# One SBUF side per MLP block, spread table loads and stage-wise schedule offsets in a fused attention, Fourier and MLP kernel

## The chip, the cores and the metric

The kernel runs on one core of one Trainium2 chip. The metric is the device time in microseconds (us), the median of three runs. A profile is one execution recorded by the hardware profiler; its engines are TensorE (PE; PEld is its weight load), VectorE (DVE), ScalarE (ACT), GpSimd (POOL) and SyncE (SP), which only issues DMAs here.

## The reference

Attention with a causal mask and a decay bias, then a block that mixes tokens with a two-dimensional Fourier transform and runs an MLP. All in float32, 8 batches, 8 heads, 576 tokens, 64 columns a head (512 in all), hidden width 2048:

```
scores = scale * q @ k.T                       # per batch and head, 576 x 576
cum = cumsum(max(s, 0));  bias = -(cum[q] - cum[k])
scores = where(causal, -1e9, scores + min(bias, 0))
attn = exp(scores - max); attn = attn / (sum(attn) + 1e-9)
x = attn @ v                                   # (8, 576, 512)
u = x + real(fft(fft(x, axis=1), axis=2))
un = (u - mean(u)) / sqrt(var(u) + 1e-6)       # over the 512 columns
out = u + max(un @ w_ch1, 0) @ w_ch2
```

## The kernel before

**Number format.** Matmuls run on float32 data in a reduced form (F32R). To keep precision a value is held as a high part and a low remainder, and a product takes three matmuls (high by high, high by low, low by high). The function split makes the pair; names ending in h and l, or indices 0 and 1, are its parts.

**Attention.** The 64 heads are worked as 32 pairs; pair i is batch i // 4, heads j = i % 4. For each pair there are steps: load fetches q and k (tile qk); high (L747 to L764) makes the high parts in the tile KQ; low (L776 to L787) makes the remainders q1 and k1 (written as q and k in the profile) and loads the values va; maxes (L802 to L832) computes scores once into pm, takes the row maxima (Mx) on VectorE, transposes them (pmt) and writes them as the row mt back into KQ; scores (L850 to L865) computes the scores ps with maxima and bias inside the product and takes the exponential into P; av (L886 to L898) multiplies by the values (pavA, pavB); recip and finish (L905 to L929) divide by the sums and write x as xa and xs. The loop over pairs interleaves the steps of neighbouring pairs with a function weave, which gives each stream a share.

**Fourier.** After every fourth pair a batch is complete. folds makes even and odd parts (De, Do); fourier multiplies them with cosine and sine tables (pzs, pzc, then pyc, pys) and writes u to DRAM (uD). Its tables are dcos, dsin, scos, ssin, each a high and a low tile, and a correction cor; load_tables (L556 to L562) issues nine transfers from Pool's queue ahead of pair i = 2. After four batches p256 (L660) adds the column 256 by nine matmuls of 290 moving columns.

**Weights.** The weights come as 64-bit numbers; rounded (L389 to L400) turns a piece of them into float32 by a chain over VectorE, ScalarE and Pool, with tiles wm, raw and we. For the first NC = 6 of the 16 blocks convert_w does this during attention and stores the result in DRAM (wD); load_w makes the pair wh, wl of block f, 128 x 1024 each, of which the first 512 columns belong to the first layer and the rest to the second.

**MLP.** The 4608 tokens are nine tiles x = 0 to 8 of 512. ln_tile loads u, gets mean and variance by matmuls with a constant (mu, var), and leaves the centred rows as uch and ucl (L459, L460). mlp_tile runs over the hidden blocks f: twelve matmuls (L497) into h with moving rows uch and ucl, then zh (ScalarE, L501) and zl (VectorE, L502), and for the block before twelve matmuls (L509 to L511) with moving rows zh and zl into four accumulators acc. At a tile's end L528 scales by r = 1 / sqrt(var), L534 to L536 add u back on Pool, and L537 stores. Tiles 0 and 1 are done in halves of eight blocks (parts k = 0 to 3) while later weights are still being made; tiles 2 to 8 are parts k = 4 to 10, each over all 16 blocks.

**Where things lie.** SBUF is given out from two ends; a pool opened with side="right" comes from the far end. Left lie lnp (u, t, th, tl), mlp0 (mu, uch, ucl, r of even tiles), zp (zh, zl), w0 and w1 (weights f < N1 = 8). Right lie, once attention and Fourier are done, wB (weights f >= 8), mlp1 (mu, uch, ucl, r of odd tiles), the stage for the conversion and op (the outputs).

**What sets the order.** The function order rebuilds the order of instructions of the program up to the end of part k = 4. It has a cost for each instruction (function cost), a model of TensorE's clock (class Clock), and times from which first inputs are held to be there (HOLD). It walks in simulated time: at each step an engine may take, of the instructions that could start within SLACK nanoseconds of the soonest, the one of least rank. The rank is the place in the program plus an offset from SHIFT, one number for each engine and name of the tile written. DMAs are held to move one after the other on a line of their issuing queue. The result is fixed as an order on every engine. Parts k > 4 are not reordered by it.

Of the kernel before, what the change touches and what calls it, by code (L numbers as in the profile page):

```python
# [55 lines left out]
SHIFT = {
    (PE, "acc"): 3291, (PE, "h"): 354, (PE, "mu"): -6, (PE, "p"): 8, (PE, "pavB"): 43, (PE, "pyc"): 54, (PE, "pys"): -23, (PE, "pzs"): -13,
    (PE, "var"): 566,
    (DVE, "Aw"): -434, (DVE, "De"): -679, (DVE, "Do"): -601, (DVE, "KQ"): 3, (DVE, "M"): -141, (DVE, "Px"): -20, (DVE, "cumhl"): -44,
    (DVE, "cw"): -401, (DVE, "e"): 160, (DVE, "eh"): 238, (DVE, "eps"): 451, (DVE, "k"): 62, (DVE, "o"): 52, (DVE, "ones"): -453, (DVE, "part"): -15,  # L60
    (DVE, "r"): 323, (DVE, "rows"): -41, (DVE, "sums"): -81, (DVE, "t"): -459, (DVE, "tl"): -439, (DVE, "trash"): -1341, (DVE, "u"): -4312,
    (DVE, "ucl"): -30, (DVE, "wbias"): -672, (DVE, "wl"): -162, (DVE, "wm"): 25, (DVE, "xr"): -154, (DVE, "ym"): -86, (DVE, "yp"): -1168,
    (DVE, "zc"): -17, (DVE, "zs"): -37,
    (ACT, "Do"): 6, (ACT, "KQ"): 2402, (ACT, "P"): 2, (ACT, "Px"): -365, (ACT, "cumhl"): -652, (ACT, "cw"): 15, (ACT, "eh"): 1013, (ACT, "mt"): 6,
    (ACT, "mu"): 59, (ACT, "part"): -533, (ACT, "r"): -28, (ACT, "rows"): -20, (ACT, "stage"): 18, (ACT, "th"): -150, (ACT, "u"): 278,
    (ACT, "we"): -154, (ACT, "yc"): 373, (ACT, "zc"): 4150, (ACT, "zh"): 739, (ACT, "zs"): 66,
    (POOL, "Bw"): -174, (POOL, "KQ"): -43, (POOL, "P"): -36, (POOL, "Px"): -10, (POOL, "dcos"): -18, (POOL, "dsin"): -24, (POOL, "ident"): 1630,
    (POOL, "o"): -72, (POOL, "q"): -5, (POOL, "scos"): -715, (POOL, "ssin"): 102, (POOL, "t"): -374, (POOL, "tri"): -12, (POOL, "trih"): 105,
    (POOL, "w"): -98, (POOL, "we"): 11, (POOL, "wl"): -321, (POOL, "xa"): -123, (POOL, "xr"): -22, (POOL, "xs"): -667,
    (SP, "KQ"): 22, (SP, "aD"): -5, (SP, "cumD"): 48, (SP, "cw"): 558, (SP, "k"): -85, (SP, "out_0_dram"): -113, (SP, "part"): -146, (SP, "qk"): 832,  # L70
    (SP, "raw"): 2317, (SP, "rb"): -1213, (SP, "rd"): -149, (SP, "rows"): 1082, (SP, "sums"): -9, (SP, "u"): 16, (SP, "uD"): -11, (SP, "wD"): -97,
    (SP, "wl"): 552, (SP, "xs"): -978,
}


# [275 lines left out]
def fused_kernel(ctx, tc, qkT, vA, sP, wP, tabD, tabS, corr, out):  # L351
    nc = tc.nc
    begin, closed = len(list(nc.all_instructions())), []
    NB = qkT.shape[0]
# [84 lines left out]
    def ln_tile(t0, n, lag):  # L439
# [12 lines left out]
        nc.scalar.copy(mu[:, :n], pm[:, :n])
# [24 lines left out]
    def mlp_tile(t0, n, lo, hi):  # L477
        uch, ucl, mu, r = LN.pop(t0) if hi == NF else LN[t0]
        last = t0 + n == NT
        x = t0 // TOK  # L480
        if last:
            w = lnp.tile([128, 4, TOK], F32, tag="u", name="u")
            for j in range(4):
                nc.gpsimd.tensor_add(w[:, j, :n], uch[:, j, :n].bitcast(F32), ucl[:, j, :n].bitcast(F32))
                nc.gpsimd.tensor_add(w[:, j, :n], w[:, j, :n], mu[:, :n])
        acc = [accp.tile([128, TOK], F32, tag=f"acc{j}", name=f"acc{j}") for j in range(4)]
        held = []
        for f in range(lo, hi + 1):
            if f < hi:
# [4 lines left out]
                i = 0  # L494
                for a, b in ((wh, uch), (wl, uch), (wh, ucl)):
                    for j in range(4):
                        nc.tensor.matmul(h[:, :n], a[:, j * 128:(j + 1) * 128], b[:, j, :n], start=i == 0, stop=i == 11)  # L497
# [44 lines left out]
    dcos = [fft.tile([128, 2, 258], F32R, name=f"dcos{i}") for i in range(2)]
    dsin = [fft.tile([128, 2, 256], F32R, name=f"dsin{i}") for i in range(2)]
    scos = [fft.tile([97, 3, 290], F32R, name=f"scos{i}") for i in range(2)]
    ssin = [fft.tile([96, 3, 290], F32R, name=f"ssin{i}") for i in range(2)]
# [9 lines left out]

    def load_tables():  # L556
        for i in range(2):
            nc.gpsimd.dma_start(out=dcos[i], in_=tabD[i, :, :, 0:258])
# [39 lines left out]
    def fourier(b, xa, xs):  # L598
# [56 lines left out]
        if b % ZB == ZB - 1:  # L655
            p = bank("p256")
            i = 0
            for c, (t0, n) in enumerate(TC):
                for x, y in PASS3:
                    nc.tensor.matmul(p[:ZB, 0:290], z256[x][:n, c], scos[y][:n, c], start=i == 0, stop=i == 8)  # L660
# [529 lines left out]
```

## Time and profile before

| | us |
|---|---|
| median of three runs | 1331.67 (1329.67 to 1333.0) |
| the profiled execution | 1331.26 |
| its span, first to last instruction | 1329.5 |
| TensorE busy | 1260.9 |
| VectorE busy | 729.0 |
| Pool busy | 549.6 |
| ScalarE busy | 543.5 |

The attention pairs run to about 472 us, the Fourier part of the last batch and the first norm to about 505; from there on the matmuls of the MLP follow one another. Tile 3 begins at about 788 us, tile 8 at 1235. In the views, a row of the busy time by stretches gives each engine's busy microseconds and count in that stretch, then the granted clock of TensorE, the mean share of the 16 DMA engines in use and GB/s. A row of the order of time gives start and length, both in us, then line, operation, written and read tiles and shape.

### The profile page before, as it was taken

Reading aid. Unit: us, or ns where it says so; the run is one execution under the profiler, and the core shown is the slowest. Engines: PE = TensorE matmul, PEld = TensorE weight load, DVE = VectorE, ACT = ScalarE, POOL = GpSimd, SP = SyncE. Lnnn points to the kernel's source line nnn. Section 1 sums busy time; section 2 is a strip of 40 time slices with the busy share of each in tenths; the row PEclk is TensorE's granted clock in tenths of the full one; section 3 lists DMA queues with packets and bytes.
Section 4 is the critical chain, followed back from the end, with each engine's and each line's share of the span. In section 5 each row is a group of like instructions: output and inputs, shape, how many; then the busy total and the mean of one; then the engine's idle time right before and its main releaser. Section 6 shows DMA issues by size and latency. Waiting matters only on the chain. (4 is left out here: it accounts for less than half of the span.)

```text
span 1329.5 us, 17949 instructions
## 1 busy us (share of the span) xinstructions
PE 1260.9 (95%) x6094; PEld 1036.0 (78%) x6094; DVE 729.0 (55%) x1659; ACT 543.5 (41%) x1220; POOL 549.6 (41%) x545
## 2 busy tenths in 40 slices
PE   5798999999999879999999999999999999999998
PEld 4677778887887758877777778888888888888886
DVE  7677897997878878787655223224224333232212
ACT  5677777777777564444232112112112121121110
POOL 5565675675767656544545031040040220430300
PEclk9999999999999999999999999999999999999999
DMA  6967666777666644334221000000000001000000
GB/s 183 218 186 188 186 177 189 203 201 181 194 177 177 167 153 163 110 119 135 74 69 54 26 24 20 22 33 32 0 32 32 16 17 32 33 0 0 32 0 32
DMA packets 76340, 129.22 MB, mean 97 GB/s; under 512 B 11620, under 2 KB 36581, under 8 KB 76249
## 3 DMA queue, kind: packets, MB, share of 16 engines
q1 hardware_dynamic: 73733, 124.01, 32.3%
q0 software_dynamic: 1696, 2.50, 1.0%
q10 hardware_dynamic: 820, 1.58, 0.4%
q8 instruction: 48, 0.79, 0.2%
q14 instruction: 43, 0.35, 0.1%
HBM read 78.94 MB, written 25.17 MB: 78 GB/s over the span
## 5 line engine op out<-in xcount | busy, mean ns | idle before, releaser
L502 DVE SCALAR_TENSOR_TENSOR zl<-h,zh 128x512 fp32r<-128x512 f32 x144 | 98.9, 687 | 390.7 <-ACT zh L501 390.6
L501 ACT ACTIVATE zh<-h 128x512 fp32r<-128x512 f32 x144 | 85.9, 597 | 506.5 <-PE h L497 404.9
L509 PE MATMUL acc<-zh,wh 128*128 128x512 f32 x576 | 226.9, 394 | 0.0
L510 PE MATMUL acc<-zh,wl 128*128 128x512 f32 x576 | 226.3, 393 | 0.0
L511 PE MATMUL acc<-zl,wh 128*128 128x512 f32 x576 | 225.6, 393 | 0.0
L886 PE MATMUL pavB<-P,va 128*128 128x320 f32 (+1 forms) x512 | 161.8, 411 | 2.2 <-DVE Mx L806 2.2
L497 PE MATMUL h<-uch,wh 128*128 128x512 f32 x576 | 159.7, 397 | 1.9 <-DVE zl L502 1.9
L497 PE MATMUL h<-ucl,wh 128*128 128x512 f32 x576 | 156.7, 393 | 0.0
L497 PE MATMUL h<-uch,wl 128*128 128x512 f32 x576 | 156.6, 393 | 0.0
L536 POOL TENSOR_TENSOR o<-o,w 128x512 f32<-128x512 f32 x32 | 42.9, 1340 | 272.5 <-issue 229.4
L853 ACT ACTIVATE P<-ps 128x320 f32<-128x320 f32 (+3 forms) x320 | 127.2, 426 | 40.2 <-PE ps L851 36.5
L802 PE MATMUL pm<-KQ 128*128 128x256 f32 (+2 forms) x352 | 115.7, 387 | 24.8 <-DVE Mx L806 12.0
L497 PEld LDWEIGHTS h<-uch,wh 128*128 128x128 f32 x576 | 106.0, 188 | 30.7 <-DVE zl L502 7.8
L511 PEld LDWEIGHTS acc<-zl,wh 128*128 128x128 f32 x576 | 108.1, 188 | 24.9
L509 PEld LDWEIGHTS acc<-zh,wh 128*128 128x128 f32 x576 | 108.2, 188 | 24.8 <-ACT zh L501 0.3
L497 PEld LDWEIGHTS h<-uch,wl 128*128 128x128 f32 x576 | 108.1, 188 | 24.9
L510 PEld LDWEIGHTS acc<-zh,wl 128*128 128x128 f32 x576 | 108.2, 188 | 24.5
L497 PEld LDWEIGHTS h<-ucl,wh 128*128 128x128 f32 x576 | 108.0, 188 | 24.4
L850 PE MATMUL ps<-KQ 128*128 128x320 f32 (+2 forms) x320 | 117.0, 373 | 7.7 <-DMA KQ<-mt 4.4
L806 DVE CUSTOM_DVE_ANT_0 trash<-pm,tri 128x192 bf16<-128x192 f32 (+3 forms) x224 | 106.0, 473 | 15.4 <-PE pm L802 6.1
L784 POOL TENSOR_TENSOR q<-qk,q 64x576 fp32r<-64x576 f32 x64 | 95.5, 1503 | 42.6 <-DMA q<-KQ 20.8
L802 PEld LDWEIGHTS pm<-KQ 128*128 128x128 f32 x352 | 65.4, 197 | 45.1 <-DVE Mx L806 22.4
(153 smaller groups left out, 2108.8 us busy)
## 6 DMA issues: line engine op xcount, KB each, us to landing
qk<-in_qkT_dram SPq DMA_DIRECT2D x32, 576.0 KB
raw<-in_wP_dram SPq DMA_DIRECT2D x64, 256.0 KB
va<-in_vA_dram SPq DMA_DIRECT2D x32, 480.0 KB
k<-KQ SPq DMA_DIRECT2D x32, 288.0 KB
q<-KQ SPq DMA_DIRECT2D x32, 288.0 KB
rb<-rd SPq DMA_DIRECT2D x64, 144.0 KB
u<-uD SPq DMA_DIRECT2D x8, 1024.0 KB
out_dram<-o SPq DMA_DIRECT2D x32, 256.0 KB
```

The lines of the kernel that those rows point to most:

```text
L497: nc.tensor.matmul(h[:, :n], a[:, j * 128:(j + 1) * 128], b[:, j, :n], start=i == 0, stop=i == 11)
L501: nc.scalar.activation(zh[:, :n], h[:, :n], AF.Relu)
L502: nc.vector.scalar_tensor_tensor(out=zl[:, :n], in0=h[:, :n], scalar=0.0, in1=zh[:, :n].bitcast(F32), op0=ALU.max, op1=ALU.subtract)
L509: nc.tensor.matmul(acc[j][:, :n], a[:, cs], y[:, :n], start=g == lo, stop=False)
L510: nc.tensor.matmul(acc[j][:, :n], b[:, cs], y[:, :n], start=False, stop=False)
L511: nc.tensor.matmul(acc[j][:, :n], a[:, cs], z[:, :n], start=False, stop=g == hi - 1)
L784: nc.gpsimd.tensor_sub(q1[64:128, h], qk[0:64, h], q1[0:64, h].bitcast(F32))
L802: nc.tensor.matmul(p[:, :w], flat(qy)[:, q:q + 128], keys, start=True, stop=True)
L806: nc.vector.tensor_tensor_reduce(out=trash[:, :n], in0=p[:, :n], in1=mask, scale=1.0, scalar=first, op0=ALU.add, op1=ALU.max, accum_out=col)
L850: nc.tensor.matmul(p[:, :n], flat(ky)[:, k0:k0 + 128], flat(qy)[:, q0 + a:q0 + a + n], start=True, stop=False)
L853: nc.scalar.activation(P[:, POFF[c] + lo:POFF[c] + hi], p[:, lo - a:hi - a], AF.Exp, scale=0.125)
L886: nc.tensor.matmul(p[:, u - lo:v - lo], va[:, c, vs], P[:, o:o + v - u], start=c == 0, stop=c == 1 and tg == "A")
```

## The change

It has these parts:

- **Sides.** From tile 2 on ln_tile writes uch and ucl always left (pool mlp0), and mlp_tile copies them by two DMAs on SP's queue to tiles of the same names on the right (pool mlp1). Blocks f < 8 read the left pair, blocks f >= 8 and the final sums the right pair. zh and zl of blocks f >= 8 lie in mlp1 as well. mu and r stay with the tile's parity. The next tile's norm starts later in a tile: after eight yields at a weight of 20, not three at 12, from part k = 4 on.
- **Tables.** dcos and dsin lie side by side in one tile dtab, scos and ssin in one tile stab (per part, high and low), and are loaded by one transfer each. load_tables(x) is called with x = 0 to 3 ahead of pairs i = 3 to 6; the last call also loads cor.
- **p256** is computed in two column ranges, 146 and 144 wide.
- **Order.** SHIFT holds seven numbers for each engine and name, chosen by a function phase from the pair (first three pairs, the pair modulo 4, three stages behind). A list SEED adds, pair by pair, a drawn offset of at most 15, 30, 60 or 120 places. SLACK is smaller for VectorE, larger for Pool and SP, and gone for ScalarE. All DMA queues share one line in the model.
- **Buffers.** The conversion of weights has two buffers in place of one in attention and behind it. A software DMA scratch is set to 4096.

```diff
-SLACK = {DVE: 26.0, ACT: 6.0, POOL: 64.0, SP: 126.0}
+SLACK = {DVE: 7.0, POOL: 83.0, SP: 140.0}
 SHIFT = {
-    (PE, "acc"): 3291, (PE, "h"): 354, (PE, "mu"): -6, (PE, "p"): 8, (PE, "pavB"): 43, (PE, "pyc"): 54, (PE, "pys"): -23, (PE, "pzs"): -13,
...
+    (PE, "acc"): (0, 0, 0, 0, 0, 0, 4380), (PE, "h"): (0, 0, 0, 0, 0, 0, 12), (PE, "mu"): (0, 13, 0, 0, 0, 0, 36),
...
 }
+SEED = (4756, 5482, 1750, 31106, 13585, 10042, 44054, 12179, 15993, 14968, 23267, 26445, 33340, 3938, 44208, 11846, 18973, 25310, 7958, 45125, 43719,
+    32797, 17108, 19408, 35945, 18022, 16488, 50522, 0, 16320, 45976, 53773, 1609, 0, 1911)
...
+def phase(k, n):
+
+    return 0 if k < 3 else 1 + k % 4 if k < n - 1 else 5 + k - (n - 1)
+
+
+def shift(k, n, engine, name):
+
+    by = SHIFT.get((engine, name), (0,) * 7)[phase(k, n)]
+    seed = SEED[k] if k < len(SEED) else 0
+    if seed:
+        draw = zlib.crc32(f"{seed} {ENGINES.index(engine)} {name}".encode()) % 2001 - 1000
+        by += math.floor(draw * (15, 30, 60, 120)[seed % 4] / 1000 + 0.5)
+    return by
...
-        s.rank = s.at + SHIFT.get((s.engine, label(s.writes[0].tensor)), 0), s.at
+        s.rank = s.at + shift(bisect.bisect(marks, s.at + first), len(marks), s.engine, label(s.writes[0].tensor)), s.at
...
-            link[e] = max(begin + 1945, link.get(e, 0.0)) + s.link
-            end = link[e] + 284
+            link = max(begin + 1945, link) + s.link
+            end = link + 284
...
@@ ln_tile
         nc.scalar.copy(mu[:, :n], pm[:, :n])
+        if t0 >= 2 * TOK:
+            mlp = mlps[0]
...
-        r = mlp.tile([128, TOK], F32, tag="r", name="r")
+        r = mlps[t0 // TOK % 2].tile([128, TOK], F32, tag="r", name="r")
...
@@ mlp_tile
+        us = [(uch, ucl)] * 2
+        if x >= 2:
+            us[1] = [mlps[1].tile([128, 4, TOK], F32R, tag=g, name=g) for g in ("uch", "ucl")]
+            for a, b in zip(*us):
+                nc.sync.dma_start(out=b.bitcast(F32), in_=a.bitcast(F32))
+            uch, ucl = us[1]
...
-                for a, b in ((wh, uch), (wl, uch), (wh, ucl)):
+                ah, al = us[f // N1]
+                for a, b in ((wh, ah), (wl, ah), (wh, al)):
...
-                zh = zp.tile([128, TOK], F32R, tag="zh", name="zh", bufs=2)
-                zl = zp.tile([128, TOK], F32R, tag="zl", name="zl", bufs=2)
+                zh = zps[f // N1].tile([128, TOK], F32R, tag="zh", name="zh", bufs=2)
+                zl = zps[f // N1].tile([128, TOK], F32R, tag="zl", name="zl", bufs=2)
...
-    def load_tables():
-        for i in range(2):
-            nc.gpsimd.dma_start(out=dcos[i], in_=tabD[i, :, :, 0:258])
-            nc.gpsimd.dma_start(out=dsin[i], in_=tabD[i, :, :, 258:514])
-            nc.gpsimd.dma_start(out=scos[i], in_=tabS[i, 0:97, 0])
-            nc.gpsimd.dma_start(out=ssin[i], in_=tabS[i, 0:96, 1])
-        nc.gpsimd.dma_start(out=cor, in_=corr)
+    def load_tables(x):
+        i = x // 2
+        if x % 2:
+            nc.gpsimd.dma_start(out=stab[i], in_=tabS[i].rearrange("p a c s -> p a (c s)"))
+        else:
+            nc.gpsimd.dma_start(out=dtab[i], in_=tabD[i])
+        if x == 3:
+            nc.gpsimd.dma_start(out=cor, in_=corr)
...
-            for c, (t0, n) in enumerate(TC):
-                for x, y in PASS3:
-                    nc.tensor.matmul(p[:ZB, 0:290], z256[x][:n, c], scos[y][:n, c], start=i == 0, stop=i == 8)
-                    i += 1
+            for lo, w in ((0, 146), (146, 144)):
+                i = 0
+                for c, (t0, n) in enumerate(TC):
+                    for x, y in PASS3:
+                        nc.tensor.matmul(p[:ZB, lo:lo + w], z256[x][:n, c], scos[y][:n, c, lo:lo + w], start=i == 0, stop=i == 8)
+                        i += 1
...
-    weights = convert_w(attb, 0, NC, 1)
+    weights = convert_w(attb, 0, NC, 2)
...
-        if i == 2:
-            load_tables()
+        if 3 <= i <= 6:
+            load_tables(i - 3)
...
-    stage, nstage = attb, 1
+    stage, nstage = attb, 2
...
         mlps.append(ctx.enter_context(pool("mlp1", side="right")))
+        zps.append(mlps[1])
...
-            streams.append([later(ln_tile(*tiles[x + 1], 1), 3), 12])
+            streams.append([later(ln_tile(*tiles[x + 1], 1), 3), 12] if k == 3 else [later(ln_tile(*tiles[x + 1], 1), 8), 20])
...
-    nc = bacc.Bacc("TRN2", target_bir_lowering=False, num_devices=1)
+    nc = bacc.Bacc("TRN2", target_bir_lowering=False, num_devices=1, dynamic_dma_scratch_size=4096)
```

More of the change, by code (lines that the diff above doesn't have):

```diff
@@ L1 @@
+import bisect
+import math
 import re
+import zlib
 from contextlib import ExitStack
@@ L54 @@
 }
-SLACK = {DVE: 26.0, ACT: 6.0, POOL: 64.0, SP: 126.0}
+SLACK = {DVE: 7.0, POOL: 83.0, SP: 140.0}
 SHIFT = {
-    (PE, "acc"): 3291, (PE, "h"): 354, (PE, "mu"): -6, (PE, "p"): 8, (PE, "pavB"): 43, (PE, "pyc"): 54, (PE, "pys"): -23, (PE, "pzs"): -13,
[L58 to L72, printed above, removed]
-}
@@ new lines @@
+    (PE, "acc"): (0, 0, 0, 0, 0, 0, 4380), (PE, "h"): (0, 0, 0, 0, 0, 0, 12), (PE, "mu"): (0, 13, 0, 0, 0, 0, 36),
+    (PE, "p"): (0, 0, 0, 0, 1941, 0, 0), (PE, "pavA"): (-89, 0, 4, 0, 0, 0, 0), (PE, "pavB"): (1476, 38, 43, 43, 46, 0, 0),
+    (PE, "pm"): (-228, 0, -6, 0, -1, 0, 0), (PE, "pmt"): (252, 0, -4047, -38, -488, 0, 0), (PE, "ps"): (-2003, 2, 1, 2, 2, 0, 0),
+    (PE, "pyc"): (0, 0, 0, 54, 53, -72, 332), (PE, "pys"): (0, 0, 0, -1186, -27, 372, -2351), (PE, "pzc"): (0, 0, 0, 0, 0, 326, 12),
@@ new lines @@
+    (PE, "pzs"): (0, 0, -12, -12, 0, 4827, 34), (PE, "var"): (0, 0, 0, 0, 0, 57, 4018),
+    (DVE, "Aw"): (363, 0, 0, 0, 0, -400, 0), (DVE, "De"): (0, 0, 0, 0, -3446, 1722, 0), (DVE, "Df"): (0, -5021, 0, 0, 34, -267, 0),
+    (DVE, "Do"): (0, 0, 0, 0, 5, 22, 0), (DVE, "KQ"): (-213, 0, 0, 0, 0, 0, 0), (DVE, "M"): (-74, -1936, -1187, -108, -97, 0, 0),
+    (DVE, "cumhl"): (199, 0, 0, 0, 0, 0, 0), (DVE, "cw"): (-170, 0, 0, 0, 0, 0, 0), (DVE, "e"): (0, 24, 0, 0, 0, -59, 0),
+    (DVE, "eh"): (-128, -147, 0, 0, 0, -15, 0), (DVE, "eps"): (47, 0, 0, 0, 0, 0, 0), (DVE, "k"): (118, -36, 22, 65, 0, 0, 0),
@@ new lines @@
+    (DVE, "o"): (0, 0, 0, 0, 0, 0, -289), (DVE, "part"): (0, 0, 0, 0, 0, 0, -28), (DVE, "r"): (0, 0, 0, 0, 0, -143, -2),
+    (DVE, "rows"): (0, 0, 0, 0, 1, 0, 0), (DVE, "sums"): (0, -69, -428, 0, 5, -1058, 0), (DVE, "t"): (0, -24, 0, 0, 0, 0, 0),
+    (DVE, "tl"): (0, 400, 0, 0, 0, -122, 0), (DVE, "trash"): (-204, -9892, -6685, -9283, -8536, 0, 0), (DVE, "u"): (0, -198, 0, 0, 0, 0, 119),
+    (DVE, "ucl"): (0, 38, 0, 0, 0, 0, -16), (DVE, "wbias"): (-49, 0, 0, 0, 0, 0, 0), (DVE, "we"): (16, 0, 199, 0, 63, 0, 62),
@@ new lines @@
+    (DVE, "wl"): (0, 0, 0, 0, 0, 2143, 49), (DVE, "wm"): (50, 0, 173, 135, 201, 0, 2729), (DVE, "xr"): (0, 0, 0, 0, 0, 129, 0),
+    (DVE, "ym"): (0, 0, 0, 0, -22, 98, -75), (DVE, "yp"): (0, 0, 0, 0, -654, 2256, 0), (DVE, "z"): (0, 0, 0, 8, 0, -95, -127),
+    (DVE, "zc"): (0, 0, -346, -606, 0, 0, -445), (DVE, "zl"): (0, 0, 0, 0, 0, 0, -995), (DVE, "zs"): (0, 0, -1990, 241, 0, -538, 145),
+    (ACT, "De"): (0, 0, 0, 0, -1180, 240, 0), (ACT, "Do"): (0, 62, 0, 0, 14, 0, 0), (ACT, "KQ"): (-37, 895, -26, 6159, 3304, 0, 0),
@@ new lines @@
+    (ACT, "P"): (-537, 0, 0, 34, 191, 0, 0), (ACT, "Px"): (0, -691, 0, 0, 0, 0, 0), (ACT, "cumhl"): (-23, 0, 0, 0, 0, 0, 0),
+    (ACT, "cw"): (376, 0, 0, 0, 0, 0, 0), (ACT, "eh"): (0, 7428, 0, 0, 0, -168, 0), (ACT, "mt"): (359, -509, 151, -718, 137, 0, 0),
+    (ACT, "mu"): (0, 627, 0, 0, 0, 0, 540), (ACT, "part"): (0, 0, 0, 0, 0, 0, -271), (ACT, "r"): (0, 0, 0, 0, 0, -146, 89),
+    (ACT, "rows"): (-644, -32, -19, 11, -4471, 92, 0), (ACT, "stage"): (176, 0, 16, 48, -5, 0, 0), (ACT, "th"): (0, 1212, 0, 0, 0, -1500, 0),
@@ new lines @@
+    (ACT, "u"): (0, 598, 0, 0, 0, 0, 0), (ACT, "uch"): (0, 950, 0, 0, 0, 0, 186), (ACT, "we"): (-35, 1758, 380, -104, -133, 0, 0),
+    (ACT, "wh"): (0, 0, 0, 0, 0, -426, 0), (ACT, "yc"): (0, 0, 0, 0, 102, -995, 0), (ACT, "zc"): (0, 0, 8611, 7059, 0, -99, 0),
+    (ACT, "zh"): (0, 0, 0, 0, 0, 0, -7), (ACT, "zs"): (0, 0, 15, 207, 0, 1509, 16),
+    (POOL, "Bw"): (0, 0, 0, 0, 24, 75, 0), (POOL, "KQ"): (109, 0, 0, 0, 0, 0, 0), (POOL, "P"): (-6, 36, 0, 0, -61, 0, 0),
+    (POOL, "Px"): (-812, 1086, 61, 0, -5669, 0, 0), (POOL, "o"): (0, 0, 0, 0, 0, 0, -528), (POOL, "q"): (-50, 1189, 30, -89, -50, 0, 0),
@@ new lines @@
+    (POOL, "stab"): (0, 0, 249, 0, 246, 0, 0), (POOL, "t"): (0, 0, 0, 0, 0, -42, 0), (POOL, "tri"): (-22, 0, 0, 0, 0, 0, 0),
+    (POOL, "we"): (0, 0, 0, -568, 0, 0, 1121), (POOL, "wl"): (0, 0, 0, 0, 0, -433, -297), (POOL, "xa"): (0, -298, 0, 0, 4, 1433, -51),
+    (POOL, "xr"): (0, 0, -70, -27, 0, 0, 0), (POOL, "xs"): (0, 0, 0, 0, -178, -470, -166),
+    (SP, "KQ"): (43, 238, 399, 1227, 53, 0, 0), (SP, "cumD"): (108, 0, 0, 0, 0, 0, 0), (SP, "cw"): (15, 0, 0, 0, 0, 0, 0),
+    (SP, "k"): (-27, 4, -82, -594, -3469, 0, 0), (SP, "part"): (0, 0, 0, 0, 0, 0, -1872), (SP, "q"): (1022, 664, 963, 1435, 1206, 0, 0),
@@ new lines @@
+    (SP, "qk"): (2721, 724, 2017, 4329, 1382, 0, 0), (SP, "raw"): (9039, 5756, 2055, 2557, 1500, 0, -46),
+    (SP, "rb"): (0, -357, -755, 43, -13, -45, 0), (SP, "rd"): (0, -322, 0, -29, -7, 0, 0), (SP, "rows"): (0, 84, 0, 0, 0, -545, 0),
+    (SP, "sums"): (-447, -247, 255, 79, 417, 224, 0), (SP, "u"): (0, 0, 0, 0, 0, 0, -139), (SP, "uD"): (0, 0, 0, 0, 1060, 73, -109),
+    (SP, "uch"): (0, 0, 0, 0, 0, 0, 160), (SP, "ucl"): (0, 0, 0, 0, 0, 0, 275), (SP, "va"): (75, 855, 1252, 66, 655, 0, 0),
+    (SP, "wD"): (0, 1082, 639, 0, -1, 0, 0), (SP, "wl"): (0, 0, 0, 0, 0, 631, 5), (SP, "xs"): (0, 0, -96, 12, 0, 31, 0),
+}
@@ L234, in run, with order @@
         return now
-def order(tc, first, last, closed):
+def phase(k, n):
[7 more added lines that the diff above has]
+    return by
+def order(tc, first, last, closed, marks):
     nc = tc.nc
@@ L280, in order @@
     at = dict.fromkeys(line, 0)
-    link, landed, taken, result = {}, [], set(), {e: [] for e in ENGINES}
+    link, landed, taken, result = 0.0, [], set(), {e: [] for e in ENGINES}
     pool = gate = 0.0
@@ L352, in fused_kernel @@
     nc = tc.nc
-    begin, closed = len(list(nc.all_instructions())), []
+    begin, closed, marks = len(list(nc.all_instructions())), [], []
     NB = qkT.shape[0]
@@ L541, in fused_kernel @@
     fft = fft_ctx.enter_context(tc.tile_pool(name="fft", bufs=1, side="right"))
[L542 to L545, printed above, removed]
+    dtab = [fft.tile([128, 2, 514], F32R, name=f"dtab{i}") for i in range(2)]
+    stab = [fft.tile([97, 2, 870], F32R, name=f"stab{i}") for i in range(2)]
+    dcos = [t[:, :, 0:258] for t in dtab]
+    dsin = [t[:, :, 258:514] for t in dtab]
+    scos, ssin = ([t[0:97 - x, x].rearrange("p (c s) -> p c s", s=290) for t in stab] for x in range(2))
     cor = fft.tile([97, 258], F32R, name="cor")
@@ L656, in fourier @@
             p = bank("p256")
-            i = 0
-            for c, (t0, n) in enumerate(TC):
-                for x, y in PASS3:
-                    nc.tensor.matmul(p[:ZB, 0:290], z256[x][:n, c], scos[y][:n, c], start=i == 0, stop=i == 8)
-                    i += 1
+            for lo, w in ((0, 146), (146, 144)):
[4 more added lines that the diff above has]
+                        i += 1
             nc.vector.tensor_add(x256[:, 0:289], x256[:, 0:289], p[:ZB, 0:289])
@@ L950, in fused_kernel @@
     for i in range(NP):
+        marks.append(traced())
         if i + 3 < NP:
@@ L986, in fused_kernel @@
             mixing = fourier(b, *xbuf.pop(b))
+    marks.append(traced())
     close(att_ctx, att)
-    zp = ctx.enter_context(pool("zp"))
+    zps = [ctx.enter_context(pool("zp"))]
     w0 = ctx.enter_context(pool("w0"))
-    stage, nstage = attb, 1
+    stage, nstage = attb, 2
     weave([later(call(recip, NP - 2), 2), 10], [later(call(finish, NP - 2), 4), 10], [av(NP - 1), AV], [mixing, FOURIER * 0.1], [norm, 6 * 0.4],
@@ L1033, in fused_kernel @@
     op = None
+    marks.append(traced())
     feed = rest()
@@ L1043, in fused_kernel @@
         if k >= 3 and x + 1 < len(tiles):
-            streams.append([later(ln_tile(*tiles[x + 1], 1), 3), 12])
+            streams.append([later(ln_tile(*tiles[x + 1], 1), 3), 12] if k == 3 else [later(ln_tile(*tiles[x + 1], 1), 8), 20])
         weave(*streams)
         if k == 4:
-            order(tc, begin, traced(), closed)
+            order(tc, begin, traced(), closed, marks)
 def take(gen, quota):
```

## The prediction

> **What bounds the kernel now.** I read the page first, then the busy time by stretches, the waits of TensorE, the chain of waits, and last single instructions.
>
> ```profile
> span 1329.5 us, 17949 instructions
> PE 1260.9 (95%) x6094; PEld 1036.0 (78%) x6094; DVE 729.0 (55%) x1659; ACT 543.5 (41%) x1220; POOL 549.6 (41%) x545
> ...
> PE h L497 22%; PE acc L511 7%; PE acc L509 7%; PE acc L510 7%; DVE o L528 0%; DVE u L530 0%; DVE r L471 0%; PE var L436 0%; PE var L435 0%; PE mu L436 0%; PE mu L435 0%; DVE zl L502 0%; DVE t L447 0%; DVEq L528 0%
> ```
>
> TensorE is the bound: busy for 95% of the span, and the chain that ended last is its MLP matmuls. Such a kernel gets faster in two ways only: fewer gaps on TensorE, or quicker matmuls. Where the gaps are, the busy time by stretches tells (each engine's microseconds, then granted clock, DMA share, GB/s):
>
> ```profile
> 0.00:20.00 20.00, 5.59 (x16) 4.08 (x17) 14.11 (x40) 8.78 (x13) 14.84 (x23) 1.00 0.57 153
> 20.00:60.00 40.00, 33.73 (x178) 27.69 (x177) 27.81 (x89) 29.93 (x73) 21.11 (x28) 1.00 0.95 219
> 60.00:100.00 40.00, 34.72 (x184) 29.19 (x183) 27.10 (x86) 27.64 (x69) 22.49 (x24) 0.91 0.73 193
> 100.00:440.00 340.00, 318.86 (x1885) 271.07 (x1884) 284.31 (x825) 255.86 (x634) 223.71 (x235) 1.00 0.68 187
> 440.00:505.00 65.00, 51.04 (x274) 43.34 (x275) 49.87 (x98) 37.01 (x89) 41.48 (x39) 0.92 0.51 157
> 505.00:736.00 231.00, 230.68 (x1028) 185.03 (x1027) 162.55 (x314) 87.21 (x181) 111.28 (x110) 1.00 0.32 104
> ```
>
> Idle on TensorE: 14.4 us before 20 us (it waits for the first inputs; I leave that alone), then 6.3, 5.3, 21.1 and 14.0 us up to 505. After that there is nearly none until the tail. The clock shares 0.91 over 40 us and 0.92 over 65 us cost another 3.6 and 5.2 us. So 55.5 us of attention time is open to a better order. After 505 only quicker matmuls help.
>
> **Operands on one side.** The tokens go through the MLP in nine tiles of 512. Each tile has 16 blocks f of 24 matmuls (12 for h, 12 for acc). Even tiles (x = 0, 2, 4, 6, 8) have their moving rows in the left pool, odd ones in the right; weight blocks f < 8 lie left, the others right; zh and zl always left. The chain of waits shows the start of each block's h group, its length and count:
>
> ```profile
> 877.36 5.46 PE h L497 x24
> ...
> 929.79 2.80 PE h L497 x12
> 935.39 2.80 PE h L497 x12
> ...
> 966.66 5.60 PE h L497 x24
> ...
> 1145.72 5.60 PE h L497 x24
> 1154.08 2.80 PE h L497 x12
> 1159.64 2.80 PE h L497 x12
> ...
> 1187.88 2.75 PE h L497 x12
> 1193.39 2.75 PE h L497 x12
> ...
> 1235.49 5.46 PE h L497 x24
> ...
> 1243.67 2.72 PE h L497 x12
> 1249.11 2.72 PE h L497 x12
> ```
>
> From start to start: tile 8, all left, 5.44 us a block (226.7 ns a matmul). Tile 4 with right weights and left rows 5.60 us (233.3 ns). Tile 7 with right rows and left weights 5.56, and with right weights, right rows but left zh and zl 5.51. The same weights f < 8 are fast under left rows and slow under right ones, and the reverse holds for the h part of f >= 8. Nothing waits in these blocks. So it is the pairing that costs, 0.16 us a block at most.
>
> After the change every block from tile 2 on has weights, rows and z on one side. A tile then takes 16 x 5.44 + 4 norm matmuls of about 0.23 = 87.96 us. Now an even one takes 966.66 - 877.36 = 89.30 and an odd one 1235.49 - 1145.72 = 89.77. Gain: tiles 2, 4 and 6, 3 x 1.34 = 4.0; tile 8, which has no next norm, 8 x 0.16 = 1.3; tiles 3, 5 and 7, 3 x 1.81 = 5.4; together 10.7 us. In the second halves of tiles 0 and 1 only z moves. Tile 1's blocks there, in order of time (start, length of the merged row):
>
> ```profile
> 656.44 1.14 PE L497 MATMUL h<-uch,wh 128*128 128x512 f32 x4
> ...
> 662.04 1.14 PE L497 MATMUL h<-uch,wh 128*128 128x512 f32 x4
> ```
>
> They take 5.60 and become one-sided: 8 x 0.16 = 1.3. Tile 0's keep their rows on the other side; I leave them at 0. Sum: 12.0 us. No block of before has all three operands right. Its best evidence, tile 7's h group there, lasts 2.75, not 2.72; if both halves of such a block took 2.75 (5.50), the eight one-sided right halves would give back 8 x 8 x 0.06 = 3.8. Between 8.2 and 12.0 I take 12: the 2.75 still holds the change-over from an acc group with z on the other side, which goes.
>
> [...]
>
> **The copies that buy it.** From tile 2 on uch and ucl are made left and copied right by two DMAs of 1 MB on SP's queue. That is new work in each of seven tiles. Rows of Pool, of the busy time by stretches, of SP's queue and of VectorE:
>
> ```profile
> 1154.06 1.29 POOL L534 TENSOR_TENSOR w<-uch,ucl 128x512 f32<-128x512 f32 x1
> 1098.00:1100.00 2.00, 2.00 (x10) 1.60 (x9) 0.77 (x2) 0.13 (x1) 0.00 (x0) 1.00 0.93 327
> 1096.38 0.38 SPq L442 DMA_DIRECT2D u<-uD  x1
> 1177.49 1.90 DVE L458 TENSOR_TENSOR u<-u,mu 128x512 f32<-128x512 f32 x3 [2.57 <-ACT mu L452]
> 1187.75 1.02 DVE L381 TENSOR_TENSOR tl<-t,th 128x512 fp32r<-128x512 f32 x1
> ```
>
> The right copy comes free when Pool has read the last slice for the tile before: 1155.35, or 9.6 us into tile 7. Two megabytes at the 327 GB/s of a u load take 6.4 us, at half of that 12.8. I estimate landing between 16 and 25 us into the tile. Block 8 reads them first at 8 x 5.44 = 43.5 us: some 18 us of cover. Without it TensorE would stand at block 8, microsecond for microsecond, once a tile. Behind the copies on SP's queue are the next u load and the tile's output stores. Tile 8's u load was issued at 1096.38, 139 us ahead of its tile, and the stores of a running tile are not due yet, so a later place in the queue hides. At 1098 the DMA engines were 0.93 busy and TensorE ran on without a gap; the copies' traffic costs nothing there.
>
> The left pair also becomes free later: the next norm may write it only after block 7's h group and the copy, about 41 us into the tile. From the first subtraction at 1177.49 to the end of the split before the second norm matmul at 1188.77 it needs 11.3 us, and the matmul stands some four blocks (21.8 us) behind the first. The rest of the tile, 47 us, covers it. I cost it at 0.
>
> **Tables.** Nine transfers from Pool's queue at the third pair become five, one in each of pairs 3 to 6 and the correction beside the last. The page, queries of single tiles, the order of time (in brackets the idle time before, and what ended it) and the busy time by stretches:
>
> ```profile
> q0 software_dynamic: 1696, 2.50, 1.0%
> L558 POOL DMA_DIRECT2D dcos<-in_tabD_dram x2: 700/702/703, 48.0 to 48.7; - x2
> 67.32 0.58 PE L861 MATMUL ps<-q,k 128*128 128x256 f32 x1 [4.15 <-POOL q L784]
> 57.98 0.39 PE L850 MATMUL ps<-KQ 128*128 128x256 f32 x1 [1.47 <-DMA KQ<-mt]
> 65.00:70.00 5.00, 2.68 (x9) 2.09 (x10) 1.84 (x4) 1.58 (x5) 4.69 (x6) 0.57 0.73 216
> L851 PE MATMUL ps<-q,k x320: 276/308/575, 22.7 to 472.0; 128*128 128x256 f32 x64, 128*128 128x320 f32 x64, 128*128 128x448 f32 x32
> 129.39 0.96 PE L616 MATMUL pzc<-dcos,De 128*97 128x258 f32 x6
> ```
>
> The 2.50 MB are issued around 48 us and the stretch 20 to 60 has the kernel's highest DMA share, 0.95. Soon after, the mt row is late by 1.5 us and the q row by 4.1, the longest wait on TensorE in mid-attention, and the clock falls to 0.57 in 65 to 70. So one place costs 4.1 us plus the 3.6 us of clock, and the 1.5 us of the mt row. The bytes stay, and four smaller bursts may delay other loads, so between 0 and 9 I take 5. The first reader of a table starts at 129.39. The 32 pairs' scores run from 22.7 to 472.0, 14.0 us a pair, so the last load, at pair 6 near 107 us, still has 20 us.
>
> **Offsets, draws, second buffers.** The waits of TensorE for the maxes (us in total, times, longest), and two rows in order of time:
>
> ```profile
> PE pm L802 <- DVE Mx L806: 12.0, 18, 1.5
> ...
> 465.37 0.55 PE L850 MATMUL ps<-KQ 128*128 128x256 f32 x1 [2.47 <-DMA KQ<-mt]
> 498.44 1.82 PE L630 MATMUL pyc<-scos,zc 96*128 96x290 f32 x6 [4.08 <-DVE z L623]
> ```
>
> These parts reorder ready instructions on every queue, and the weight conversion gets a second buffer, so that its load no longer waits for the chain before it; the planner's one line for all DMA queues and its smaller slacks are of the same kind. No instruction's length changes, so the bound is idle time: what is left of 55.5 after the tables' 9 is 46 us. Most of it is small (18 waits of pm for the maxes make 12.0 us) and a reordering usually trades one small wait for another; the large single ones, z 4.1 and mt 2.5, stand in the stretch 440 to 505, where a wait also costs clock. I take 8: these two and 1.4 of the clock. Bounds: 20 gained, or 5 lost if the planned lengths mislead it.
>
> **The p256 sum** is cut from 9 matmuls of 290 columns into 18 of 146 and 144, twice in the kernel:
>
> ```profile
> 340.48 1.43 PE L660 MATMUL p<-scos,z 97*4 97x290 f32 x9
> ```
>
> As many columns for 0, or twice the time for 2 x 1.43 = 2.9. I take 1.
>
> **Sum.** -12 - 5 - 8 + 1 = -24 us. The profiled execution took 1331.26, 0.4 under the median of 1331.67. 1331.3 - 24 = 1307, and with the 0.4, 1308 us.
>
> **Rivals.** (1) The new order gives nothing on the chip: the gaps move, the tables' traffic with them. For it: the planner's lengths are fixed numbers, and the 12.0 us are 18 pieces. Against: the 4.1 us at 67 stands right behind the burst. Time: 1331.7 - 12 + 1 = 1321, between 1316 and 1325. (2) The side isn't the cause; tile parity or something else that moves with it is, and the copies bring nothing: 1331.7 - 5 - 8 + 1 = 1320, between 1312 and 1325. Against: both weight sets change their speed with the rows. [...] (3) The change doesn't do what it says, because the copies land late: the 24 us are eaten when each of seven tiles stalls 3.4 us, that is when they land 47 us into the tile: 1332. Only another wait ahead of them on SP's queue brings that. (4) Slower: in every pair the new order puts a pm matmul ahead of the maxes that free its bank, and TensorE, which takes its list in order, stands there. One more such wait a pair at today's 12.0 / 18 = 0.67 us makes 32 x 0.67 = 21; 1331.7 - 12 + 1 + 21 = 1342. It decides (4 us slower) from 0.47 us a pair on. For it: VectorE is as busy as 284 of 340 us between 100 and 440. Against: those waits are few now.
>
> **Numbers.** Forecast 0.62, (1) 0.17, (2) 0.06, (3) 0.07, (4) 0.08. About 0.3% (4 us) is what a measurement of this kernel can tell from no change. Faster: 0.62 + 0.17 + 0.06 = 0.85; same 0.07; slower 0.08. The forecast's own range is 1296 to 1319: 12 + 4 + 20 = 36 us at best, 8.2 + 5 (tables) + 1 (order) - 1 (p256) = 13 at worst; the further bounds need several luckier or worse terms at once. Taking in (1) and (2), it is 1296 to 1324.
>
> **What would show it.** Blocks of 5.44 us throughout from tile 2 on, tile starts 88.0 apart; copies landed before block 8, with no wait of h on a DMA; the clock at 1.00 between 60 and 100 and no 4 us wait for a q row; TensorE's idle time before the end of attention down from 61 us by about 10. Wrong would be: right-hand blocks still at 5.5 or more, a wait at block 8 or at the norm matmuls, or attention ending no earlier than 505.

## The result, and the profile after

| | us, median | runs | ratio to before, 95% interval |
|---|---|---|---|
| before | 1331.93 | 4 | |
| changed | 1312.76 | 4 (1310.2 to 1319.14) | 0.9865 (0.9828 to 0.9903) |
| changed, timed again beside before | 1312.81 | 6 | 0.9888 (0.9868 to 0.9908) |

The change makes the kernel faster by 19 us in the first timing and by some 15 in the second; the two intervals reach from 12 to 23 us. Forecast were 24 us and a time of 1308, with a range from 1296 to 1324. The total lies inside the range; several of its parts did not come as forecast, as the experiments show.

The page of the changed kernel:

```profile
span 1310.4 us, 17964 instructions
PE 1250.2 (95%) x6112; PEld 1037.0 (79%) x6112; DVE 727.4 (56%) x1659; ACT 542.5 (41%) x1220; POOL 546.5 (42%) x541
```

TensorE is busy 10.7 us less with 18 more matmuls (the p256 cut) at nearly the same mean granted clock (0.993 before, 0.992 now), so the matmuls are quicker. The rest of the 19.1 us of span is idle time. The busy time by stretches of the changed kernel, columns as before:

```profile
20.00:60.00 40.00, 38.06 (x212) 31.67 (x211) 30.66 (x102) 33.71 (x85) 19.09 (x25) 1.00 0.80 210
60.00:100.00 40.00, 34.45 (x184) 27.34 (x182) 25.95 (x85) 26.66 (x66) 22.72 (x25) 1.00 0.87 219
100.00:440.00 340.00, 318.76 (x1876) 273.52 (x1876) 285.58 (x824) 253.95 (x633) 225.10 (x236) 0.98 0.69 188
440.00:505.00 65.00, 57.56 (x310) 48.27 (x309) 57.35 (x103) 37.84 (x90) 46.95 (x43) 0.95 0.58 182
505.00:736.00 231.00, 228.93 (x1031) 184.72 (x1030) 153.71 (x297) 85.46 (x176) 104.23 (x103) 1.00 0.30 102
```

Two stretches gained busy time: 20 to 60 (33.73 us busy before, 38.06 now) and 440 to 505 (51.04, now 57.56), in all 10.9 us. The stretch from 60 to 100 gained clock instead, 0.91 before and 1.00 here. The long middle gained nothing: 318.86 before, 318.76 now, and the clock there fell from 1.00 to 0.98. The chain of waits of the changed kernel shows the MLP (start of an h group, its length, its count):

```profile
1129.26 5.46 PE h L546 x24
1137.45 2.72 PE h L546 x12
1142.89 2.72 PE h L546 x12
...
1198.34 2.72 PE h L546 x12
1203.78 2.72 PE h L546 x12
1209.22 2.72 PE h L546 x12
1217.38 5.46 PE h L546 x24
```

Blocks are 5.44 us apart in the left half (1137.45 to 1142.89) and in the right half (1203.78 to 1209.22), and tile 8 starts 88.12 us after tile 7. Before, tiles were 89.30 and 89.77 apart. Tile 3 starts at 776.98 us, where it was 787.82: 10.8 us are gained ahead of it and 8.3 behind it.

### The profile page after: what moved, and what is told of

Its sections match the earlier page's. It is cut to its first block, busy times and chain, and to the rows that moved or that the text cites. A ratio compares the mean times of both kernels' runs of the same rounds, so it can differ in the third digit from the quotient of the medians.

```text
span 1310.4 us, 17964 instructions
## 1 busy us (share of the span) xinstructions
PE 1250.2 (95%) x6112; PEld 1037.0 (79%) x6112; DVE 727.4 (56%) x1659; ACT 542.5 (41%) x1220; POOL 546.5 (42%) x541
## 5 line engine op out<-in xcount | busy, mean ns | idle before, releaser
L903 PE MATMUL ps<-q,k 128*128 128x320 f32 (+2 forms) x320 | 99.8, 315 | 0.0
```

The lines of the kernel that those rows point to most:

```text
L903: nc.tensor.matmul(p[:, :n], flat(k1)[:, k0:k0 + 128], flat(q1)[:, q0 + a:q0 + a + n], start=False, stop=True)
```

## The experiments

Theory A: operands on one side make quicker blocks, which gives the larger half, and the order gives the rest. Theory B, its rival: something else that goes with tile parity makes the slow blocks, and the order gives all. Two more came up on the way: C, a copy of mu in ScalarE's list holds up the MLP, and D, the bytes of the tables delay small transfers wherever the loads are put.

All ratios are to the kernel before, on the same chip. Its median there was 1329.3 to 1330.4 us.

| kernel | us, median | ratio, 95% interval |
|---|---|---|
| sides alone | 1327.33 | 0.9986 (0.9972 to 1.0001) |
| sides alone, mu with two buffers | 1320.99 | 0.9942 (0.9921 to 0.9962) |
| changed without sides | 1320.96 | 0.9943 (0.9922 to 0.9964) |
| changed, z on the other side | 1326.33 | 0.9984 (0.9965 to 1.0003) |
| the same, mu with two buffers | 1321.03 | 0.9950 (0.9933 to 0.9966) |
| changed with the old offsets | 1340.21 | 1.0092 (1.0068 to 1.0116) |
| changed without draws | 1310.48 | 0.9868 (0.9846 to 0.9890) |
| tables alone | 1335.69 | 1.0051 (1.0028 to 1.0075) |
| changed, all tables at pair 2 | 1338.50 | 1.0074 (1.0046 to 1.0103) |
| changed, p256 in nine matmuls | 1326.39 | 0.9979 (0.9959 to 0.9998) |
| changed, no draws, mu with two buffers | 1313.32 | 0.9885 (0.9860 to 0.9911) |

**The changed kernel again.** No edit.

> The changed kernel unaltered, timed beside the others on their chip. 1311 to 1313, 18 to 20 us below before.

1312.81 us, as expected, though only 16.5 below before on that chip where 18 to 20 were expected. It is the measure for the three kernels timed beside it: z on the other side with two mu buffers, p256 in nine matmuls, and no draws with two mu buffers.

**Sides alone, and everything but the sides.** The first puts the sides part (ln_tile, mlp_tile, the pools and the later norm, with the smaller scratch) into the kernel before; the second takes it out of the changed kernel. Each keeps the attention order of the kernel that it comes from.

> The kernel before with the sides part alone (left and right rows and z, the copies, the later norm, the smaller software scratch); its order of attention is that of before, instruction for instruction. Theory A (operands on one side are quicker, and this is the larger half of the gain): tiles 88.1 us apart, 11 us below before, 1321. Theory B (something else that goes with tile parity makes the 5.60 us blocks, and the gain comes from the order alone): tiles still 89.3 and 89.8 apart, 1332. If the copies disturbed something it would be above 1332.

> The changed kernel without the sides part; its order of attention is that of the changed kernel. Theory A: tiles 89.3 and 89.8 apart again, 11 us above the changed kernel, 1324, which leaves 8 us for the order, the tables and the buffers together. Theory B: 1313, as changed.

The chain of waits without the sides part, first h group of tiles 4 to 6:

```profile
871.70 5.46 PE h L537 x24
961.00 5.60 PE h L537 x24
1050.77 5.46 PE h L537 x24
```

Tiles are 89.30 and 89.77 us apart again, and the kernel is slower than the changed one by 0.9943 - 0.9888, some 7 us (11 were expected). Theory B falls: the tables were untouched, and up to 527 us every engine has its instructions in the order of the changed kernel. But the sides alone brought only 0.14%, where 11 us were expected. Something took the gain back. ScalarE in order of time (in brackets its idle time before, and what ended it), then TensorE, then the busy time by stretches of that kernel:

```profile
789.35 0.60 ACT L510 ACTIVATE zh<-h 128x512 fp32r<-128x512 f32 x1 [7.82 <-PE h L506]
797.62 0.58 ACT L452 COPY mu<-mu 128x512 f32<-128x512 f32 x1 [7.66 <-POOL w L544]
798.10 1.09 ACT L510 ACTIVATE zh<-h 128x512 fp32r<-128x512 f32 x2
```

```profile
798.75 0.50 PE L518 MATMUL acc<-zh,wh 128*128 128x512 f32 x1 [1.28 <-ACT zh L510]
801.93 0.79 PE L520 MATMUL acc<-zl,wh 128*128 128x512 f32 x1 [2.45 <-DVE zl L511]
```

```profile
790.00:800.00 10.00, 8.21 (x35) 6.14 (x34) 2.44 (x4) 1.57 (x3) 8.45 (x7) 1.00 0.41 155
800.00:810.00 10.00, 8.07 (x23) 6.38 (x24) 2.48 (x5) 0.00 (x0) 2.55 (x2) 0.66 0.34 135
```

At tile 3 the mu copy of tile 4 stands in ScalarE's list ahead of a zh. It waits 7.66 us for Pool, which still reads tile 2's mu (L544). The zh behind it waits too, TensorE stands for 3.7 us, and then its clock is halved for a while: 0.66 of full speed over the next 10 us.

**A second buffer for mu.** If that is the cause, mu needs only another buffer:

```diff
-        mu = mlp.tile([128, TOK], F32, tag="mu", name="mu")
+        mu = mlp.tile([128, TOK], F32, tag="mu", name="mu", bufs=2)
```

> The kernel with the sides part alone, and a second buffer for mu in both pools. Theory C: with the sides alone the gain of quicker matmuls is there (tiles 88.1 us apart), but 7 us of it are lost once, at tile 3, where the mu copy of tile 4 stands in ScalarE's list ahead of a zh and waits for Pool's last read of tile 2's mu; TensorE waits 3.7 us and its clock is halved for 6.8 us. With the second buffer that wait has nothing to wait for: 7 us under the run with sides alone, 1320, and no half-clock stretch near 780 to 800 us. Rival: the half clock there comes from something else (the copies' traffic), then it stays and the time is 1327.

1320.99 us, where 1320 was expected. ScalarE's rows at that place, the stretch and the tile starts (chain of waits):

```profile
790.35 0.60 ACT L510 ACTIVATE zh<-h 128x512 fp32r<-128x512 f32 x1 [7.82 <-PE h L506]
793.07 0.60 ACT L510 ACTIVATE zh<-h 128x512 fp32r<-128x512 f32 x1 [2.12 <-PE h L506]
```

```profile
800.00:810.00 10.00, 10.00 (x46) 8.29 (x45) 0.69 (x1) 1.20 (x2) 2.58 (x2) 1.00 0.43 170
```

```profile
875.25 5.47 PE h L506 x24
963.37 5.46 PE h L506 x24
```

No copy stands between the zh, the clock stays at 1.00, and tiles are 88.12 apart. The sides are worth 0.58% (0.38 to 0.79), or 7.7 us, in the old order, much as in the new one, once this wait is out of the way. The changed kernel doesn't have the wait: there tile 4's second mu matmul stands at 817.6 us, long after Pool is done (797.4 us). The traces show what goes with the wait: where it came (sides alone, z on the other side with one buffer, the old offsets), both mu matmuls of tile 4 ran before tile 3 began, at 746 to 764 us; in the kernel before (818.3) and in the changed one the second ran well inside tile 3, and the copy after it. Why the same program text gives the lists another order there I didn't settle, so it is luck that the changed kernel has no such wait.

**z on the other side.** Only zh and zl move, from tile 2 on:

```diff
-                zh = zps[f // N1].tile([128, TOK], F32R, tag="zh", name="zh", bufs=2)
+                zh = zps[(f // N1) ^ (x >= 2)].tile([128, TOK], F32R, tag="zh", name="zh", bufs=2)
```

(and zl likewise), once with one and once with two buffers for mu.

> The changed kernel, but from tile 2 on zh and zl lie on the other side than the weights they meet; nothing else moves. Theory A: the 12 acc matmuls of a block go from 2.72 to about 2.80 us and the first matmuls behind them a little too, a block from 5.44 to about 5.53; 112 blocks make 10 us, 1323. Theory B: no change, 1313.

> The changed kernel with zh and zl on the other side from tile 2 on, and two buffers for mu. Theory A and C together: no half clock at tile 3, tiles 89.7 us apart, 7 x 1.57 = 11 us above the changed kernel, 1323, and 4 to 7 us under the run with the same z and one mu buffer (1326 there). Rival to C: the half clock at tile 3 stays.

The chain of waits of the second kernel, tile 8, left blocks and right blocks:

```profile
1236.78 2.76 PE h L546 x12
1242.34 2.76 PE h L546 x12
...
1281.20 2.75 PE h L546 x12
1286.74 2.75 PE h L546 x12
```

Blocks take 5.56 and 5.54 us in place of 5.44, with the weights, the rows uch and ucl and the transfers where they were; from tile 5 on TensorE, VectorE and Pool have their instructions in the same order in both kernels. So the side of the moving rows against the weights is the cause, which settles theory A. The run moves only the acc half of a block; for the h half there are the blocks of the kernel before and of the changed one. What in SBUF makes its two ends differ, no run shows. Counted from the first zh of tile 3 to the end of the span, the part without table loads or attention, the profiles give 538.9 us before, 538.9 without the sides, 530.7 changed, 530.4 with the sides and two mu buffers in the old order, and 539.9 here. The kernel with one buffer showed the half clock at tile 3 again (0.81 and 0.85 from 790 to 810), the one with two did not (1.00), and the second buffer brought some 5 us. Against the changed kernel the one with two buffers is 8.2 us slower; 11 were expected.

**The order.** The changed kernel, with the old offsets and slacks and no draws; and with the new stage offsets but no draws.

```diff
-    by = SHIFT.get((engine, name), (0,) * 7)[phase(k, n)]
+    by = SHIFT.get((engine, name), 0)
-    seed = SEED[k] if k < len(SEED) else 0
+    seed = 0
```

> The changed kernel planned with the old offsets (one per engine and name), the old slacks and no draws; tables, buffers, sides and the one line for DMA queues as changed. Theory A with the order as the source of the other 8 us: 6 to 8 us above the changed kernel, 1320, with the idle time of TensorE before 505 us near 58 us again. Rival: the tables and the second buffers are the source, then 1313 to 1315 and idle time near 51 us.

> The changed kernel without the drawn offsets, stage offsets as changed. If the draws are worth something on the chip: 3 to 8 us above the changed kernel, 1316 to 1321, spread over all pairs. Rival: they fit the planner's lengths only, then within 2 us, 1311 to 1315.

With the old offsets the kernel is slower than before: 1340.21. That run has the wait of tile 3 too, for which I estimate some 6 us from the sides alone with one and two mu buffers (0.9986 against 0.9942), but its last score matmul starts at about 481 us, where it was 472.0 before and 463.6 in the changed kernel. Its longest waits of TensorE (us in total, times, longest):

```profile
PE acc L540 <- DVE zl L531: 8.4, 2, 6.0
PE pzs L639 <- ACT Do L400: 7.7, 2, 7.5
```

Neither was there before. The old offsets belong to the old list of instructions; put on the new one they make new single waits. The draws bring nothing that can be measured: 1310.48 without, 1312.8 with, intervals that overlap. So the 30 us between these two kernels belong to the stage offsets and slacks, the estimated 6 us at tile 3 among them. The second conversion buffers, the one line for all DMA queues in the model and the smaller scratch were not run by themselves.

**The tables.** Alone in the kernel before; and in the changed kernel, but all four at pair 2:

```diff
-        if 3 <= i <= 6:
-            load_tables(i - 3)
+        if i == 2:
+            for y in range(4):
+                load_tables(y)
```

> The kernel before with the tables part alone: merged tiles, five transfers at pairs 3 to 6, the smaller software scratch; the old offsets replanned. Theory D: the bytes of the tables delay small transfers on the same DMA engines wherever they lie, so spreading moves the loss from 60 us to 80 and 110 us and brings 0 to 4 us: 1326 to 1330. My prediction's step: 5 us gained, 1325. If the old offsets do not fit the new place of the loads, it is slower than before, up to 1338.

> The changed kernel with its four merged table loads all at pair 2, offsets and draws as changed, replanned. Theory D: TensorE's lead over before is lost near 60 us and not at 80 to 110; the sum differs by 0 to 4 us from the changed kernel, 1313 to 1317. If the draws are fitted to one plan and any other is worse, as the run with old offsets suggests, 1320 or more, and the loss lies in pairs whose table loads did not move.

Alone the part makes the kernel slower, 0.5%. In order of time on TensorE:

```profile
93.18 0.38 PE L831 MATMUL pmt<-ident,Mx 128*9 128x128 f32 x1 [3.54 <-DVE Mx L808]
103.19 0.58 PE L852 MATMUL ps<-KQ 128*128 128x256 f32 x1 [2.43 <-DMA KQ<-mt]
```

The waits of before at 58 and 67 us are gone, and these are there: the second on a small transfer, the first on a VectorE that had itself stood 2.85 us for one (sums, at 91.29 us). Busy time by stretches, before and with the tables alone:

```profile
0.00:75.00 75.00, 50.18 (x240) 40.85 (x241) 49.11 (x149) 44.90 (x101) 43.85 (x60) 0.95 0.80 192
75.00:110.00 35.00, 32.41 (x184) 27.34 (x183) 25.66 (x82) 27.64 (x70) 18.10 (x22) 1.00 0.76 204
```

```profile
0.00:75.00 75.00, 54.28 (x271) 43.86 (x272) 54.27 (x165) 48.93 (x113) 41.10 (x55) 1.00 0.72 191
75.00:110.00 35.00, 27.89 (x143) 23.41 (x143) 21.32 (x64) 22.83 (x56) 18.55 (x24) 0.90 0.96 213
```

TensorE is 31 matmuls ahead at 75 us and 10 behind at 110. So the loss moved, as theory D has it; that the bytes do it, and not the new order of the instructions, is not shown apart. This makes the part worth nothing, but not 5 us slower. A new wait does stand far behind the last table load, right after attention:

```profile
507.32 0.80 PE L435 MATMUL mu<-th,ones 128*128 128x512 f32 x1 [6.64 <-ACT th L380]
```

TensorE takes 4 matmuls from 500 to 508 us, where it took 38 before, and its clock is 0.67 from 508 to 520. The kernel before has no such wait there, and the last table load was issued at 95 us, so it comes with the replanned order and not with the bytes. In the changed kernel, too, the loss lies behind the loads, which it issues between 53 and 96 us (busy time by stretches):

```profile
80.00:100.00 20.00, 18.61 (x103) 14.95 (x102) 12.45 (x42) 14.78 (x35) 10.62 (x12) 1.00 0.84 215
100.00:120.00 20.00, 15.57 (x72) 13.05 (x73) 12.35 (x33) 13.07 (x35) 11.45 (x12) 0.83 0.79 199
```

With all loads at pair 2 the loss comes at once and is larger (order of time, then busy time by stretches):

```profile
61.52 1.62 PE L938 MATMUL pavA<-P,va 128*128 128x256 f32 x4 [6.39 <-DMA va<-in_vA_dram]
```

```profile
40.00:60.00 20.00, 12.49 (x62) 10.57 (x62) 11.02 (x32) 9.96 (x25) 8.75 (x13) 0.91 1.16 226
60.00:80.00 20.00, 15.38 (x60) 11.91 (x61) 8.96 (x33) 9.05 (x22) 5.42 (x7) 0.76 0.40 104
```

A values load lands 6.4 us late, TensorE idles 7.5 of 20 us and then runs at 0.76. From 40 to 60 us it does 62 matmuls, and the changed kernel 116. VectorE's 46th write of Mx stands at 82.6 us, in the changed kernel at 63.7, so most of the loss is there by then. The whole is 25.7 us slower than the changed kernel, where theory D had 0 to 4. Both undoings also replan everything behind the loads, so each price is that of the place and of a plan together: in the new order the spread is worth much, in the old one less than nothing.

**p256 in nine matmuls.** The two column ranges become one again.

> The changed kernel with the p256 sum in nine matmuls of 290 columns again. Its own price is nothing: 18 took 1.40 us in the changed kernel's trace and 9 took 1.43 before. But the plan of every instruction behind the first p256 is another one. Price alone: within 1 us of the changed kernel. If any replanning that the offsets were not made for costs as in the runs with old offsets or tables at pair 2, 3 to 10 us slower.

The price in place is nil, as the row of the changed kernel shows (18 matmuls; nine took 1.43 before):

```profile
527.55 1.40 PE L712 MATMUL p<-stab,z 97*4 97x146 f32 x18
```

Yet the kernel is 13.6 us slower than the changed one. With nine instructions fewer in the list, every offset counted in places meets another list from the first p256 on. (TensorE's instructions follow one another as in the changed kernel up to 340 us, those of VectorE, ScalarE and Pool up to 350.) Its stretch at the end of attention:

```profile
440.00:505.00 65.00, 53.56 (x286) 45.26 (x285) 45.19 (x89) 36.02 (x87) 39.20 (x39) 0.92 0.47 147
```

4.0 us less busy than in the changed kernel, at a lower clock. The last score matmul stands at 473.0 us in place of 463.6, and the first zh of tile 3 at 798.9 in place of 779.8; this profiled execution took 1331.28, 4.9 above the median of its kernel. Which instruction's place does it I didn't find.

**Without draws, with two mu buffers.** Meant as the best of both.

> The changed kernel without draws and with two buffers for mu. The changed kernel has no stall at tile 3 for the second buffer to remove, so 0 to 3 us under the changed kernel, 1308 to 1312.

1313.32 us, no better than the changed kernel: without a stall at tile 3 there is nothing for the buffer to remove.

## Why the prediction was right and where it was wrong

- **Operands on one side, 12 us.** Right in mechanism and nearly in size. The right-hand blocks run at 5.44, not 5.50, as I took it. From tile 3 on 9.4 us were forecast and 8.3 measured: a tile takes 88.12 us, not 87.96. As a whole the part measured 7.3 us (taken out) and 7.7 (put in, with the second mu buffer). The 2.6 us forecast for tile 1's second half and tile 2 don't show in these sums, and they are the larger part of the 4 to 5 us by which the term was too large.
- **Copies at 0.** Right in the changed kernel. For tile 8 the first copy was issued 9.7 us into the tile, as worked out, and Pool's first read of both copies started 17.7 us in (16 to 25 forecast):

```profile
L532 POOL TENSOR_TENSOR u<-uch,ucl x4: 1285/1287/1288, 1235.1 to 1241.3; 128x512 f32<-128x512 f32 x4
L527 SPq DMA_DIRECT2D uch<-uch x1: 470/470/470, 1227.1 to 1227.1; - x1
```

- **The later norm at 0.** This step was incomplete. I covered uch and ucl and forgot mu, which keeps its pool and has one buffer. With the sides alone its copy blocked ScalarE's list and cost some 6 us (some 5 with z on the other side); which of the sides' edits brought tile 4's second mu matmul forward is not shown. That the changed kernel escapes it is luck, for the prediction did not ask. Asking what is queued behind each new wait on its engine finds it: a zh.
- **Tables, -5.** Wrong as a term by itself: alone it is 5.3 us slower (1335.69 against 1330.37). The profile of before showed the loss behind the burst rightly, but the sum took it as removed by half, while TensorE's lead at 75 us was gone again at 110. That makes 0. The longest new wait, 6.6 us at 507, comes with the replanned order, and the term had no price for replanning.
- **Offsets, -8.** Order, tables and buffers together brought 0.57% (0.36 to 0.78), 7.6 us, where the terms -5, -8 and +1 made -12. The place was right: at the end of attention both waits that I had named (z 4.1 and mt 2.5) are gone, though a new one of h for yp, 5.1 us, stands there. But the size says little, since the term has no value without the others: on the same list the stage offsets are worth 30 us against the old ones.
- **p256, +1.** In place 0. As an undo, 13.6 us.
- **Rivals.** (1), the order gives nothing, is refuted by the kernel without sides at 0.9943. (2) is refuted by the z runs. (3) and (4) did not come in the changed kernel; the mechanism of (4), an instruction placed ahead of what it waits for, did come with the old offsets, on ScalarE and at single places rather than in each pair.
- **Signs.** The clock at 1.00 between 60 and 100 came in the first execution, and the half clock went to 110 us (0.66 from 110 to 120); in the one timed again the clock was 0.96 there. Idle time before 505 fell from 61 to 50.6 us as said; the clock lost 0.02 x 340 + 0.05 x 65 = 10.1 us there, against 8.8 before.

Forecast were 12 us for the sides and 12 for the rest; measured were 7.5 and 7.6, and 15 to 19 for the whole. Both terms were too large, and the range held them. The range was narrower than its terms: its best case counts 4 us for the tables and its worst 5, where the term's own bounds were 9 and 0. With every term at its own bound it would have gone from about 1291 to 1331. That the measured time lies within 5 us of 1308 is in part luck: alone, the tables went the other way, and the offsets' 8 us were a guess that no run prices by itself.

## What to carry to other kernels

Put moving rows and the weights that they meet on one side of SBUF (here 5.44 us a block against 5.60); find such a cost by comparing blocks of the same instructions that differ in where one operand lies. When a buffer is moved or freed later, list every tile of that pool that stays single, and what stands behind its writer on its engine. With an order planned from offsets, a part of the change that alters the planned list has no value of its own: take the plan and the list it was made for as one thing, and expect that a small edit can cost as much as a large one. The sides, which leave the order of attention alone, kept their value in both plans.
